# A three-stage kernel on one Trainium2 core: the second MLP's denominator as a linear step squared on GpSimd, and a new order of all instructions

## The chip, the cores and the metric

The kernel runs on one core of a Trainium2 chip. The metric is the device time of one execution in microseconds (us). The kernel before takes 1487.1 us, the median of three runs (1486.95 to 1488.85). A profile of one execution is available. In it PE is TensorE (matmuls; PEld its weight loads), DVE is VectorE, ACT is ScalarE, POOL is GpSimd and SP is SyncE, which issues the transfers. `L949` is line 949 of the kernel.

## What is computed

Attention of 12288 tokens (128 channels) against 768 pooled keys, then two MLPs of 128 to 2048 to 128. The first squares a ReLU, the second applies a rational function P/Q to every element of its hidden layer:

```python
s = scale * (q @ k.T);  a = softmax(s);  x = a @ v          # attention
g = maximum(x @ w1_in, 0) ** 2;          x = g @ w1_out      # first MLP
h = x @ w2_in                                               # second MLP
P = a[0] + a[1] * h + a[2] * h**2 + a[3] * h**3
Q = 1.0 + abs(b[0]) * abs(h) + abs(b[1]) * h**2
out = (P / (Q + 1e-06)) @ w2_out
```

## The kernel before, in words

**Tiling.** The tokens are cut into 25 batches: one of 384, 22 of 512, one of 384 and one of 256. For each batch the work is attention (`attention`), then 16 chunks of the first MLP (`mlp1`, a chunk being 128 rows of the hidden layer), then 8 pairs of chunks of the second MLP (`mlp2`). Most matmuls are done as three fp32r matmuls on high and low parts (L805 to L807 for the input sides, L823 to L825 for the output side of chunks that are split), the rest as one fp32 matmul, which the trace lists as two records (L819).

**The elementwise work of a pair in the second MLP.** With u = |h| from ACT (L944), Q is made in one of two ways. For the pairs in `qpool` (0, 1, 3, 4, 5 and 7) GpSimd makes `K = s1*u + s2` (L947) and then `K = K*u` (L949), and ACT takes `Ln(K + dp)` (L969). For the other two pairs ACT makes `K = (s*u + k1)^2` in one instruction (L952) and takes `Ln(K + da)`. Then ACT makes y0 = exp(-ln) (L970), a first guess of 1/Q, into PSUM. DVE makes P from a square by ACT (L958) with L960, and combines guess and P in three steps: L982 (P times the guess), L984 (Q times the guess) and L987 (one Newton step and the product). Pairs 0 and 3 (`spl`) are split into mH (ACT L997 or DVE L998) and mL (POOL L1000). In the first MLP a chunk goes through ReLU (ACT L847 or DVE L850), a square (POOL L856, in place and of a tile with itself, or ACT L853), and, for split chunks, gH (ACT L865) and gL (POOL L871). L779, L782 and L785 split each MLP's input (x and y) into high and low parts; L785 with `yl` in it is what the second MLP of a batch has to wait for.

**What sets the order.** No loop nest does. `Plan` collects all operations with priorities (a due time by batch and chunk, plus the entry of `off` for the operation's name), penalties for each of two possible engines (`sq_act`, `sq_pool` and the like), the costs `c_dve`, `c_actp`, `c_pool` and so on, the number of buffers (`bufs`) and the most PSUM banks that a kind of tile may hold at once (`caps`; `h2` is the second MLP's hidden layer). `order()` plays them forward and gives one fixed sequence to each engine. On the chip each engine then runs its own sequence strictly in order, waiting on semaphores.

The whole program exists twice, the second time for coefficients out of range (`TERMS`). Only the first (`SQUARES`, `fast`) runs here. The columns of `co_f` hold the coefficients: `k1`, `k2`, `dp`, `da`.

Of the kernel before, what the change touches and what calls it, by code (L numbers as in the profile page):

```python
# [14 lines left out]
ALU = mybir.AluOpType  # L15
# [3 lines left out]
QS = 2.0 ** -20  # L19
QC = QS * (1.0 + 1e-6)  # L20

PE, ACT, DVE, POOL, DMA = "PE", "ACT", "DVE", "POOL", "DMA"
# [10 lines left out]
    hs=[0, 1, 3, 4, 5],  # L33
    lo_dve=60,
    bufs=dict(
        qr=1, qh=1, ql=1, e=4, mn=17, sm=21, aT=1, xh=2, xl=1, yh=2, yl=2, aH=3, aL=2, g1=8, U=2, K=3, Z=7, o=1,
        gH=6, gL=3, mH=1, mL=1,
    ),
    caps=dict(
        h2=6, yb=5, sc=6, st=6, x=1, h1=5, y1=1, y2=1, dc=1,  # L40
    ),
    lead1=17.5,
    leada=18.0,
    d1=3,
    d2=3,
    g=2,
    pair=('kk', 'qp', 'sq2', 'ln', 'y0', 'g0', 'tt', 'rr', 'g2', 'ml', 'mh'),
    rem=[],
    md_act=1,
    md_dve=60,  # L50
    rl_act=8,
    rl_dve=2,
    qh_act=4,
    qh_dve=1,
    spd=[],
    spl=[0, 3],
    qpool=[0, 1, 3, 4, 5, 7],
    sq_act=8,
    sq_pool=0.5,
    gh_act=0.5,  # L60
    gh_dve=60,
    mh_act=8,
    mh_dve=0,
    ml_pool=0,
    ml_dve=60,
    ev_dve=8,
    hi_dve=0,
    rg=1,
    low=4,
    avs=5,  # L70
# [1 line left out]
    head=[384],  # L72
    tail=[384, 256],
    off=dict(
        mh2=-266.25, mh1=-79.25, sc=-10.0, tr=0.75, nr=-368.25, g2=7.0, ex=-137.5, kk=-177.25, rl=-4.75,
        tt=85.5, ev=79.75, mo2=10.5, ln=49.75, g0=-38.25, ab=3.5, sq=184.75, y0=14.75, mn=-278.0, qp=100.0,
        av=-119.5, mo1=4.25, sP=85.5, sq2=132.5, rr=198.5, mh=-16.5, ml=-198.75,
    ),
    free=150.0,
)  # L80
# [10 lines left out]
        qr=1, qh=1, ql=2, e=4, mn=9, sm=5, aT=1, xh=2, xl=2, yh=2, yl=2, aH=3, aL=3, g1=7, U=2, K=2, Z=5, o=1,  # L91
        gH=5, gL=3, mH=3, mL=2,
    ),
    caps=dict(
        dc=6, h2=5, yb=4, sc=5, st=3, x=1, h1=5, y1=1, y2=1,
    ),
    lead1=22.0,
# [5 lines left out]
    rem=[],  # L103
    md_act=0,
    md_dve=0,
    rl_act=2,
    rl_dve=60,
    qh_act=0,
    qh_dve=0.5,
    spd=[],  # L110
    spl=[],
    qpool=[],
    sq_act=4,
    sq_pool=2,
    gh_act=0.5,
# [3 lines left out]
    ml_pool=8,  # L119
    ml_dve=0.5,  # L120
    ev_dve=60,
    hi_dve=1,
# [8 lines left out]
        kk=-27.5, rl=59.75, tt=-37.5, ev=-109.0, mo2=4.25, ln=66.5, g0=-61.0, ab=-105.5, sq=289.5, y0=5.0,  # L131
        mn=-287.5, qp=-77.0, av=-156.0, mo1=5.75,
# [18 lines left out]


def c_mm3(n):
    return 3 * (0.4375 * n + 6)


def c_mm4(n):
# [22 lines left out]

def c_pool(n):
    return 157 + 2.105 * n


def c_pools(n):
# [183 lines left out]
def program(ctx, tc, CFG, fast, co, room, wsr, qT, kvT, w1_in, w1_out, w2_in, w2_out, outT):  # L369

    nc = tc.nc
# [10 lines left out]
    NB = len(sizes)  # L382
# [57 lines left out]
    w_hi = [const.tile([128, DFF], F32R, name=f"w{m}h") for m in range(2)]  # L440
    w_lo = [const.tile([128, DFF], F32R, name=f"w{m}l") for m in range(2)]

    REM, SPL, SPD, QPOOL = CFG["rem"], CFG["spl"], CFG["spd"], CFG["qpool"]
    HS = [[fi for k in ks for fi in (2 * k, 2 * k + 1)] for ks in (CFG["hs"], sorted(REM + SPL + SPD))]
    place = [{fi: n for n, fi in enumerate(x for x in range(NF) if x not in HS[m])} for m in range(2)]
    w_o = [const.tile([128, max(1, len(place[m])), C], F32, name=f"w{m}o") for m in range(2)]
# [439 lines left out]
    def mlp2(b, fp, p):  # L886
        T = sizes[b]
        key = lambda n: [(n, b, fp, e) for e in range(G)]
        hh, yy, uu, ku, zz, mh_, ml_ = (key(n) for n in ("h2", "yb", "U", "K", "Z", "mH", "mL"))
        rem, spl, spd, qpool = fp in REM, fp in SPL, fp in SPD, fp in QPOOL or not fast  # L890

        def add(name, alts, new=None, rd=(), wr=()):

# [48 lines left out]
        def one(name, eng, cost, go, *args, **kw):  # L942
            add(name, [(eng, cost, go, 0)], *args, **kw)
        one("ab", ACT, c_actp, lambda v: act(out=v(uu), in_=v(hh), func=AF.Abs), "U", [hh])  # L944
        if qpool:
            s1, s2 = (QS, co["k2"]) if fast else (co["b"][:, 1:2], co["b"][:, 0:1])
            one("kk", POOL, c_pools, lambda v: ts(  # L947
                out=v(ku), in0=v(uu), scalar1=s1, scalar2=s2, op0=ALU.mult, op1=ALU.add), "K", [uu])
            one("qp", POOL, c_pool, lambda v: nc.gpsimd.tensor_tensor(  # L949
                out=v(ku), in0=v(ku), in1=v(uu), op=ALU.mult), None, [uu], [ku])  # L950
        else:
            one("sq2", ACT, ptr(c_acts), lambda v: act(  # L952
                out=v(ku), in_=v(uu), func=AF.Square, scale=QS ** 0.5, bias=co["k1"]), "K", [uu])
        dl = (co["dp"] if qpool else co["da"]) if fast else QC
        dl_ap = dl if fast else co["qc"]
        c_dl = ptr(c_dve) if fast else c_dve
        if fast:
            one("sP", ACT, ptr(c_actp), lambda v: act(  # L958
                out=v(zz), in_=v(hh), func=AF.Square, bias=co["c"]), "Z", [hh])
# [118 lines left out]
@with_exitstack  # L1078
def attn_moe_moe(
    ctx: ExitStack,  # L1080
    tc: tile.TileContext,
    qT: bass.AP,
    kvT: bass.AP,
    w_sr: bass.AP,
    w1_in: bass.AP,
    w1_out: bass.AP,
    w2_in: bass.AP,
    w2_out: bass.AP,
    pa: bass.AP,
    pb: bass.AP,  # L1090
    outT: bass.AP,
):

    nc = tc.nc
    pool = ctx.enter_context(tc.tile_pool(name="coef", bufs=1))
    wsr = pool.tile([128, w_sr.shape[1]], F32, name="wsr")  # L1100
    room = pool.tile([128, room_size(SQUARES)], F32, name="room")
    col = lambda n, name: pool.tile([128, n], F32, name=name)
    ab, m, r, v, t, w = col(6, "ab"), col(6, "m"), col(2, "r"), col(3, "v"), col(8, "t"), col(6, "w")
    co_f, co_g, flag = col(8, "cf"), col(8, "cg"), pool.tile([128, 1], I32, name="flag")
    c1 = lambda x, n: x[:, n:n + 1]
    nc.sync.dma_start(out=ab[:, 0:4], in_=pa.to_broadcast([128, 4]))
    nc.sync.dma_start(out=ab[:, 4:6], in_=pb.to_broadcast([128, 2]))
    nc.sync.dma_start(out=wsr, in_=w_sr)
    n = KC * kvT.shape[2]
    for c in range(kvT.shape[1] // KC):  # L1110
        nc.sync.dma_start(out=room[:, c * n:(c + 1) * n].rearrange("p (k r) -> p k r", k=KC),
                          in_=kvT[:, c * KC:(c + 1) * KC, :])
    nc.scalar.preload_act_table_set("natural_log_exp_and_others")
    V = nc.vector

    def ts(out, in0, s1, s2, op0, op1=None):
        V.tensor_scalar(out=out, in0=in0, scalar1=s1, scalar2=s2, op0=op0, **({} if op1 is None else dict(op1=op1)))
    MUL, ADD, SUB, MAX, MIN = ALU.mult, ALU.add, ALU.subtract, ALU.max, ALU.min
    GE, LE = ALU.is_ge, ALU.is_le

    V.scalar_tensor_tensor(out=m, in0=ab, scalar=-1.0, in1=ab, op0=MUL, op1=MAX)
    V.tensor_reduce(out=c1(t, 0), in_=m[:, 0:4], axis=AX.X, op=MAX)

    ts(c1(t, 1), c1(t, 0), c1(m, 3), 16.0, MUL, MUL)
    ts(c1(t, 2), c1(m, 2), c1(m, 2), None, MUL)
    V.tensor_tensor(out=c1(w, 0), in0=c1(t, 2), in1=c1(t, 1), op=LE)

    V.scalar_tensor_tensor(out=c1(w, 1), in0=c1(t, 0), scalar=2.0 ** -20, in1=c1(m, 3), op0=MUL, op1=LE)
    ts(c1(w, 2), c1(t, 0), 2.0 ** -40, None, GE)
    ts(c1(w, 3), c1(t, 0), 2.0 ** 40, None, LE)  # L1130

    ts(c1(t, 3), c1(m, 4), c1(m, 4), 0.25, MUL, MUL)
    V.tensor_tensor(out=c1(w, 4), in0=c1(t, 3), in1=c1(m, 5), op=LE)
    ts(c1(t, 4), c1(m, 5), 2.0 ** 10, None, LE)
    V.scalar_tensor_tensor(out=c1(w, 5), in0=c1(m, 5), scalar=2.0 ** -10, in1=c1(t, 4), op0=GE, op1=MUL)
    V.tensor_reduce(out=c1(t, 5), in_=w, axis=AX.X, op=MIN)
    V.tensor_copy(out=flag, in_=c1(t, 5))
    fits = nc.values_load(flag[0:1, 0:1], min_val=0, max_val=1)

    ts(c1(t, 6), c1(t, 5), -1.0, 1.0, MUL, ADD)  # L1140
    V.scalar_tensor_tensor(out=c1(r, 0), in0=c1(ab, 3), scalar=c1(t, 5), in1=c1(t, 6), op0=MUL, op1=ADD)
    V.scalar_tensor_tensor(out=c1(r, 1), in0=c1(m, 5), scalar=c1(t, 5), in1=c1(t, 6), op0=MUL, op1=ADD)
    V.reciprocal(out=r, in_=r)
    ts(v, ab[:, 0:3], c1(r, 0), None, MUL)
    ts(c1(co_f, 0), c1(v, 2), 0.5, None, MUL)
    V.scalar_tensor_tensor(out=c1(co_f, 1), in0=c1(co_f, 0), scalar=c1(co_f, 0), in1=c1(v, 1), op0=MUL, op1=SUB)
    ts(c1(t, 7), c1(m, 4), c1(r, 1), 0.5, MUL, MUL)
    ts(c1(co_f, 2), c1(t, 7), QS ** 0.5, None, MUL)
    ts(c1(co_f, 3), c1(t, 7), 2.0 * QS, None, MUL)
    ts(c1(co_f, 4), c1(r, 1), QC, None, MUL)  # L1150
    V.scalar_tensor_tensor(out=c1(co_f, 5), in0=c1(co_f, 2), scalar=c1(co_f, 2), in1=c1(co_f, 4), op0=MUL, op1=SUB)
    ts(c1(co_f, 5), c1(co_f, 5), -1.0, None, MUL)
    ts(c1(co_f, 6), c1(ab, 3), c1(r, 1), QS, MUL, MUL)

    ts(co_g[:, 0:4], ab[:, 0:4], QS, None, MUL)
    ts(co_g[:, 4:6], m[:, 4:6], QS, None, MUL)
    V.memset(c1(co_g, 6), QC)
    args = (room, wsr, qT, kvT, w1_in, w1_out, w2_in, w2_out, outT)
    with tc.If(fits > 0) as branch:
        with ExitStack() as c:  # L1160
# [46 lines left out]
```

## Time and profile before

| | |
|---|---|
| median of three runs | 1487.1 us |
| the profiled execution | 1486.9 us |
| its span, first to last instruction | 1484.7 us |
| PE busy | 1439.5 us, 97% |
| ACT busy | 1393.4 us, 94% |
| DVE busy | 1386.9 us, 93% |
| POOL busy | 1334.1 us, 90% |

The profiled execution took 2.2 us more than its span. Busy is the time in which an engine has an instruction under way. Matmul records overlap, since a matmul starts before the last has drained; how much work PE is given is therefore read from the distance between the starts of matmuls that follow one another without a wait, and not from their lengths.

### The profile page before, as it was taken

What the parts mean: (1) busy time and instruction counts of PE and PEld (TensorE: products, weight loads), DVE (VectorE), ACT (ScalarE), POOL (GpSimd) and SP (SyncE); (2) the same over time, 40 slices, a digit from 0 to 9 for tenths busy, and PEclk for the clock granted to TensorE, in tenths of its full rate; (3) what the DMA queues carried; (4) which work ended last, traced back from release to release, by engine and by line L of the source; (5) the groups of instructions that cost most, each with busy time, mean ns of one, the idle gap of its engine ahead of it and who ended that gap; (6) DMA issues with size and microseconds to landing.
All of it is one profiled execution on the core that took longest, in us unless ns stands there. A gap on an engine that the chain in (4) does not pass through costs nothing.

```text
span 1484.7 us, 18746 instructions
## 1 busy us (share of the span) xinstructions
PE 1439.5 (97%) x5991; PEld 1053.8 (71%) x5991; DVE 1386.9 (93%) x1857; ACT 1393.4 (94%) x2318; POOL 1334.1 (90%) x1021
## 2 busy tenths in 40 slices
PE   5999999999999999999999999999999999999986
PEld 4887767766767777776777777777777777767764
DVE  7999999999999999999999999999989899989998
ACT  3789989999999999999999999999999999999996
POOL 4789999998999899999998997989999999889984
PEclk8999999999999999999999999999999999999998
DMA  7310000000000000000000000000000000000000
GB/s 283 114 36 8 13 0 15 14 2 8 15 8 15 8 3 13 15 8 8 8 15 8 1 15 15 8 8 15 8 8 8 8 13 1 11 5 3 8 8 12
DMA packets 15549, 28.62 MB, mean 19 GB/s; under 512 B 1745, under 2 KB 6737, under 8 KB 15441
## 3 DMA queue, kind: packets, MB, share of 16 engines
q1 hardware_dynamic: 15440, 27.34, 5.5%
q8 instruction: 49, 0.80, 0.2%
q14 instruction: 60, 0.48, 0.1%
HBM read 21.04 MB, written 6.29 MB: 18 GB/s over the span
## 4 chain that ended last, share of the span: by engine, by line
PE 67%; POOL 13%; ACT 8%; DVE 7%; issue 3%; DMA 1%; SPq 0%; POOLq 0%; ACTq 0%; DVEq 0%
PE psum L819 17%; PE psum L805 9%; PE psum L806 8%; PE psum L807 8%; PE psum L679 4%; PE psum L824 4%; POOL room L949 4%; PE psum L825 4%; PE psum L823 4%; PE psum L720 4%; POOL gL L871 3%; POOL room L947 2%; POOL room L856 2%; PE psum L750 1%; PE psum L749 1%
## 5 line engine op out<-in xcount | busy, mean ns | idle before, releaser
L949 POOL TENSOR_TENSOR room<-room 128x1024 f32<-128x1024 f32 (+2 forms) x150 | 348.3, 2322 | 3.6
L871 POOL TENSOR_TENSOR gL<-room,gH 128x512 fp32r<-128x512 f32 (+2 forms) x250 | 313.0, 1262 | 20.8 <-PE psum L824 15.8
L960 DVE SCALAR_TENSOR_TENSOR room<-room,cf,psum 128x512 f32<-128x512 f32 (+2 forms) x400 | 279.5, 720 | 17.4 <-ACT room L958 15.8
L819 PE MATMUL psum<-room,w1o 128*128 128x512 f32 (+2 forms) x600 | 285.2, 583 | 4.0 <-DVE room L987 4.0
L856 POOL TENSOR_TENSOR room<-room 128x512 f32<-128x512 f32 (+2 forms) x261 | 262.3, 1022 | 12.5 <-ACT room L847 6.6
L982 DVE SCALAR_TENSOR_TENSOR room<-room,v,psum 128x1024 f32<-128x1024 f32 (+2 forms) x200 | 246.1, 1232 | 21.2 <-ACT psum L970 19.4
L958 ACT ACTIVATE room<-psum,cf 128x512 f32<-128x512 f32 (+2 forms) x400 | 262.8, 688 | 0.0
L969 ACT ACTIVATE room<-room,cf 128x1024 f32<-128x1024 f32 (+2 forms) x200 | 226.3, 1132 | 25.4 <-POOL room L949 24.8
L984 DVE SCALAR_TENSOR_TENSOR psum<-room,cf,psum 128x1024 f32<-128x1024 f32 (+2 forms) x200 | 247.5, 1238 | 0.0
L987 DVE SCALAR_TENSOR_TENSOR room<-psum,room 128x1024 f32<-128x1024 f32 (+2 forms) x200 | 235.2, 1177 | 3.1
L944 ACT ACTIVATE room<-psum 128x512 f32<-128x512 f32 (+2 forms) x400 | 223.4, 593 | 12.5 <-PE psum L807 6.5
L947 POOL TENSOR_SCALAR room<-room,cf 128x1024 f32<-128x1024 f32 (+2 forms) x150 | 164.7, 1098 | 48.3 <-ACT room L944 36.0
L970 ACT ACTIVATE psum<-room 128x1024 f32<-128x1024 f32 (+2 forms) x200 | 202.7, 1015 | 0.7 <-DVE room L960 0.3
L805 PE MATMUL psum<-yh,w1h 128*128 128x512 f32 (+2 forms) x400 | 191.2, 478 | 4.8 <-DVE room L987 3.5
L805 PE MATMUL psum<-xh,w0h 128*128 128x512 f32 (+2 forms) x400 | 182.8, 457 | 1.6 <-DVE xh L782 1.2
L819 PEld LDWEIGHTS psum<-room,w1o 128*128 128x128 f32 x600 | 111.1, 192 | 63.1 <-issue 42.9
L806 PE MATMUL psum<-xl,w0h 128*128 128x512 f32 (+2 forms) x400 | 153.4, 383 | 1.5 <-DVE xl L785 1.2
L807 PE MATMUL psum<-yh,w1l 128*128 128x512 f32 (+2 forms) x400 | 154.2, 386 | 0.0
L806 PE MATMUL psum<-yl,w1h 128*128 128x512 f32 (+2 forms) x400 | 153.9, 385 | 0.0
L807 PE MATMUL psum<-xh,w0l 128*128 128x512 f32 (+2 forms) x400 | 153.6, 384 | 0.0
L847 ACT ACTIVATE room<-psum 128x512 f32<-128x512 f32 (+2 forms) x255 | 148.3, 601 | 5.1 <-PE psum L807 3.2
L865 ACT ACTIVATE gH<-room 128x512 fp32r<-128x512 f32 (+2 forms) x250 | 149.8, 632 | 2.9 <-POOL room L856 2.6
(126 smaller groups left out, 3124.4 us busy)
## 6 DMA issues: line engine op xcount, KB each, us to landing
room<-in_kv_dram SPq DMA_DIRECT2D x16, 384.0 KB, 7.8
room<-in_q_dram SPq DMA_DIRECT2D x22, 256.0 KB, 2.6
out_dram<-room SPq DMA_DIRECT2D x22, 256.0 KB, 2.0
room<-in_moe_w_in_dram SPq DMA_DIRECT2D x8, 512.0 KB, 4.6
room<-in_moe_w_out_dram SPq DMA_DIRECT2D x16, 256.0 KB, 2.7
room<-in_q_dram SPq DMA_DIRECT2D x2, 192.0 KB, 4.7
out_dram<-room SPq DMA_DIRECT2D x2, 192.0 KB, 1.9
room<-in_q_dram SPq DMA_DIRECT2D x1, 128.0 KB, 2.0
```

What stands on the lines that cost most here:

```text
L805: nc.tensor.matmul(out=out, lhsT=w_hi[m][:, sl], rhs=hi, start=True, stop=False)
L806: nc.tensor.matmul(out=out, lhsT=w_hi[m][:, sl], rhs=lo, start=False, stop=False)
L807: nc.tensor.matmul(out=out, lhsT=w_lo[m][:, sl], rhs=hi, start=False, stop=True)
L819: nc.tensor.matmul(out=o, lhsT=w_o[m][:, place[m][fi], :], rhs=rhs(), start=first, stop=last)
L856: nc.gpsimd.tensor_tensor(out=G(), in0=G(), in1=G(), op=ALU.mult)
L871: nc.gpsimd.tensor_tensor(out=mk("gL", gl)[:, :T], in0=G(), in1=f(tiles[gh][:, :T]), op=ALU.subtract)
L949: one("qp", POOL, c_pool, lambda v: nc.gpsimd.tensor_tensor(out=v(ku), in0=v(ku), in1=v(uu), op=ALU.mult), None, [uu], [ku])
L958: one("sP", ACT, ptr(c_actp), lambda v: act(out=v(zz), in_=v(hh), func=AF.Square, bias=co["c"]), "Z", [hh])
L960: one("z3", DVE, ptr(c_dve), lambda v: stt(out=v(zz), in0=v(zz), scalar=co["nd"], in1=v(hh), op0=ALU.subtract, op1=ALU.mult), None, [hh], ...
L982: one("g0", DVE, ptr(c_dve), lambda v: stt(out=v(zz), in0=v(zz), scalar=e0, in1=v(yy), op0=ALU.add, op1=ALU.mult), None, [yy], [zz])
L984: one("tt", DVE, c_dl, lambda v: stt(out=v(yy), in0=v(ku), scalar=dl, in1=v(yy), op0=ALU.add, op1=ALU.mult), None, [ku], [yy])
L987: one("g2", DVE, c_dve, lambda v: stt(out=v(g_), in0=v(yy), scalar=2.0, in1=v(zz), op0=ALU.subtract, op1=ALU.mult, reverse0=True), None, [ ...
```

## The change

In the second MLP the two GpSimd steps of a pair become `K = sqrt(QS)*u + k1` and `K = K*K`: the second step takes one tile twice where it took two tiles. The constant that is left to `Ln` and to L984 is then `da` for all pairs, and `k2` and `dp` go (the column of `dp` is kept, since `da` is made from it). The number of instructions of a pair stays. The first step keeps its form, one multiplication and one addition per element.

The pairs that take the GpSimd way in the last two batches (384 and 256 tokens) are `qtail` (0, 3, 4, 5, 6 and 7): pair 6 in the place of pair 1.

The planner has a new cost for the second step (`c_poolq`), and its numbers are new: penalties, due times, buffers, caps. `c_mm3` gets a lower bound of 110, which no size of this kernel reaches.

```diff
-        qr=1, qh=1, ql=1, e=4, mn=17, sm=21, aT=1, ...
-        gH=6, gL=3, mH=1, mL=1,
+        qr=1, qh=1, ql=1, e=5, mn=27, sm=29, aT=1, ...
+        gH=5, gL=3, mH=1, mL=1,
-        h2=6, yb=5, sc=6, st=6, x=1, h1=5, y1=1, y2=1, dc=1,
+        h2=4, yb=6, sc=6, st=5, x=1, h1=6, y1=1, y2=1, dc=1,
-    lead1=17.5,
+    lead1=20.5,
+    qtail=[0, 3, 4, 5, 6, 7],
-    sq_act=8,
-    sq_pool=0.5,
+    sq_act=0,
+    sq_pool=8,
...
-        mh2=-266.25, mh1=-79.25, ...
+        mh2=-164.5, mh1=-75.5, ...
...
+def c_poolq(n):
+    return 1.96 * n + 10
...
-        rem, spl, spd, qpool = fp in REM, fp in SPL, fp in SPD, fp in QPOOL or not fast
+        rem, spl, spd, qpool = fp in REM, fp in SPL, fp in SPD, not fast or fp in (QPOOL if b < NB - 2 else QTAIL)
...
-            s1, s2 = (QS, co["k2"]) if fast else (co["b"][:, 1:2], co["b"][:, 0:1])
+            s1, s2 = (QS ** 0.5, co["k1"]) if fast else (co["b"][:, 1:2], co["b"][:, 0:1])
...
-            one("qp", POOL, c_pool, lambda v: nc.gpsimd.tensor_tensor(
-                out=v(ku), in0=v(ku), in1=v(uu), op=ALU.mult), None, [uu], [ku])
+            qf = ku if fast else uu
+            one("qp", POOL, c_poolq if fast else c_pool, lambda v: nc.gpsimd.tensor_tensor(
+                out=v(ku), in0=v(ku), in1=v(qf), op=ALU.mult), None, [uu], [ku])
...
-        dl = (co["dp"] if qpool else co["da"]) if fast else QC
+        dl = co["da"] if fast else QC
```

**POOL, in the middle of the program, before** (a row is a line, an operation, out<-in and its size; x3 stands for three alike in a row; `room` holds most working tiles):

```order
L947 TENSOR_SCALAR room<-room,cf 128x1024
L856 TENSOR_TENSOR room<-room 128x512
L949 TENSOR_TENSOR room<-room 128x1024
L871 TENSOR_TENSOR gL<-room,gH 128x512
L947 TENSOR_SCALAR room<-room,cf 128x1024
L856 TENSOR_TENSOR room<-room 128x512
L949 TENSOR_TENSOR room<-room 128x1024
L871 TENSOR_TENSOR gL<-room,gH 128x512 x2
L856 TENSOR_TENSOR room<-room 128x512 x3
L1000 TENSOR_TENSOR mL<-room,mH 128x1024
```

Now, at about the same place (L953 and L956 are the two steps of Q, L862 the first MLP's square, L877 gL):

```order
L953 TENSOR_SCALAR room<-room,cf 128x1024
L877 TENSOR_TENSOR gL<-room,gH 128x512
L956 TENSOR_TENSOR room<-room 128x1024
L877 TENSOR_TENSOR gL<-room,gH 128x512
L862 TENSOR_TENSOR room<-room 128x512
L953 TENSOR_SCALAR room<-room,cf 128x1024
L877 TENSOR_TENSOR gL<-room,gH 128x512
L956 TENSOR_TENSOR room<-room 128x1024
L862 TENSOR_TENSOR room<-room 128x512
L877 TENSOR_TENSOR gL<-room,gH 128x512
L862 TENSOR_TENSOR room<-room 128x512
L1007 TENSOR_TENSOR mL<-room,mH 128x1024
```

The kinds of instructions are the same; other work now stands between the two steps of Q, and over the whole program 22 more squares of 512 columns stand on POOL and 22 fewer on ACT.

**DVE at the end, before**, from the split of the last batch's y (256 tokens) on; the rows of 384 belong to the batch ahead of it:

```order
L785 TENSOR_TENSOR yl<-psum,yh 128x256
L984 SCALAR_TENSOR_TENSOR psum<-room,cf,psum 128x2x384
L960 SCALAR_TENSOR_TENSOR room<-room,cf,psum 128x384 x2
L987 SCALAR_TENSOR_TENSOR room<-psum,room 128x2x384
L982 SCALAR_TENSOR_TENSOR room<-room,v,psum 128x2x384
L984 SCALAR_TENSOR_TENSOR psum<-room,cf,psum 128x2x384
L987 SCALAR_TENSOR_TENSOR room<-psum,room 128x2x384
L982 SCALAR_TENSOR_TENSOR room<-room,v,psum 128x2x384
L960 SCALAR_TENSOR_TENSOR room<-room,cf,psum 128x384 x2
L984 SCALAR_TENSOR_TENSOR psum<-room,cf,psum 128x2x384
L987 SCALAR_TENSOR_TENSOR room<-psum,room 128x2x384
L982 SCALAR_TENSOR_TENSOR room<-room,v,psum 128x2x384
```

Now (L791 is that split; L967, L989, L991 and L994 are L960, L982, L984 and L987):

```order
L791 TENSOR_TENSOR yl<-psum,yh 128x256
L991 SCALAR_TENSOR_TENSOR psum<-room,cf,psum 128x2x384
L967 SCALAR_TENSOR_TENSOR room<-room,cf,psum 128x384 x2
L994 SCALAR_TENSOR_TENSOR room<-psum,room 128x2x384
L989 SCALAR_TENSOR_TENSOR room<-room,v,psum 128x2x384
L991 SCALAR_TENSOR_TENSOR psum<-room,cf,psum 128x2x384
L994 SCALAR_TENSOR_TENSOR room<-psum,room 128x2x384
L989 SCALAR_TENSOR_TENSOR room<-room,v,psum 128x2x384
L967 SCALAR_TENSOR_TENSOR room<-room,cf,psum 128x256 x3
L991 SCALAR_TENSOR_TENSOR psum<-room,cf,psum 128x2x384
L989 SCALAR_TENSOR_TENSOR room<-room,v,psum 128x2x256
```

Behind the split stood 6 pairs' worth of L984 and of L987 at 384 columns, 5 of L982, 8 of L960 and one cast (L998); now it is 3, 3, 2, 2 and none. The rest stands ahead of the split. Those of 256 columns, all behind it, are the same in number. On PE likewise: behind the last output matmul of the first MLP, 12 chunks of the batch of 384 still had their input matmuls to come (L805 to L807), now 2.

## Rows read from the trace of the kernel before

**Rows 1.** The page: span and busy time of each engine

```profile
span 1484.7 us, 18746 instructions
PE 1439.5 (97%) x5991; PEld 1053.8 (71%) x5991; DVE 1386.9 (93%) x1857; ACT 1393.4 (94%) x2318; POOL 1334.1 (90%) x1021
```

**Rows 2.** Stretches: their length, each engine's busy us (instructions), then the granted clock

```profile
0.00:47.40 47.40, 28.54 (x141) 24.76 (x141) 38.95 (x96) 18.47 (x36) 21.15 (x27) 0.86 0.66 236
47.40:107.60 60.20, 59.67 (x301) 50.83 (x302) 58.15 (x131) 53.13 (x115) 52.45 (x56) 1.00 0.26 82
107.60:1412.00 1304.40, 1295.93 (x5316) 936.89 (x5315) 1226.00 (x1541) 1262.91 (x2049) 1215.02 (x898) 1.00 0.03 9
1412.00:1432.90 20.90, 20.09 (x103) 15.88 (x102) 19.59 (x25) 19.93 (x42) 20.28 (x22) 1.00 0.04 13
1432.90:1484.70 51.80, 35.27 (x135) 25.48 (x133) 44.21 (x68) 38.98 (x81) 25.22 (x22) 0.82 0.03 9
1469.70:1480.00 10.30, 7.93 (x23) 6.10 (x24) 9.37 (x16) 5.89 (x12) 3.19 (x3) 0.51 0.01 2
```

**Rows 3.** The timeline of PE in the middle: start, length, instruction

```profile
610.79 0.60 PE L720 MATMUL psum<-ident,room 128*128 128x128 f32 x4
611.23 1.88 PE L819 MATMUL psum<-room,w1o 128*128 128x512 f32 x4
...
700.28 0.39 PE L807 MATMUL psum<-yh,w1l 128*128 128x512 f32 x1
700.50 0.39 PE L805 MATMUL psum<-yh,w1h 128*128 128x512 f32 x1
...
709.64 1.88 PE L819 MATMUL psum<-room,w1o 128*128 128x512 f32 x4
710.96 0.80 PE L823 MATMUL psum<-gH,w0oh 128*128 128x512 f32 x1
711.59 0.40 PE L824 MATMUL psum<-gL,w0oh 128*128 128x512 f32 x1
```

**Rows 4.** POOL's and ACT's groups by shape: count, busy us, mean ns, idle before

```profile
L949 POOL TENSOR_TENSOR room<-room 128x1024 f32<-128x1024 f32 x132 | 318.5, 2413 | 2.7
L871 POOL TENSOR_TENSOR gL<-room,gH 128x512 fp32r<-128x512 f32 x220 | 284.6, 1304 | 18.2 <-PE psum L824 14.5
L856 POOL TENSOR_TENSOR room<-room 128x512 f32<-128x512 f32 x232 | 241.5, 1057 | 12.3 <-ACT room L847 6.6 <-DVE room L850 1.9
L949 POOL TENSOR_TENSOR room<-room 128x512 f32<-128x512 f32 x6 | 7.7, 1286 | 0.5
L856 POOL TENSOR_TENSOR room<-room 128x256 f32<-128x256 f32 x14 | 8.6, 637 | 0.2
L853 ACT ACTIVATE room<-room 128x512 f32<-128x512 f32 x120 | 74.6, 649 | 1.0 <-DVE room L850 0.8
```

**Rows 5.** Waits: engine, line, whom it waited for; us in total, times, longest

```profile
ACT room L969 <- POOL room L949: 24.8, 43, 1.7
PEld psum L805 <- DVE room L960: 12.1, 35, 1.2
PE psum L819 <- DVE room L987: 4.0, 4, 1.3
```

**Rows 6.** The timeline of DVE near the end: start, length, instruction, idle before

```profile
1433.17 0.42 DVE L785 TENSOR_TENSOR yl<-psum,yh 128x256 fp32r<-128x256 f32 x1
1433.51 1.01 DVE L984 SCALAR_TENSOR_TENSOR psum<-room,cf,psum 128x768 f32<-128x768 f32 x1
1434.43 0.61 DVE L960 SCALAR_TENSOR_TENSOR room<-room,cf,psum 128x384 f32<-128x384 f32 x1
1435.20 0.61 DVE L960 SCALAR_TENSOR_TENSOR room<-room,cf,psum 128x384 f32<-128x384 f32 x1 [0.16 <-ACT room L958]
1435.73 0.95 DVE L987 SCALAR_TENSOR_TENSOR room<-psum,room 128x768 f32<-128x768 f32 x1
1436.60 1.00 DVE L982 SCALAR_TENSOR_TENSOR room<-room,v,psum 128x768 f32<-128x768 f32 x1
```

More of the change, by code (lines that the diff above doesn't have):

```diff
@@ L35 @@
     bufs=dict(
-        qr=1, qh=1, ql=1, e=4, mn=17, sm=21, aT=1, xh=2, xl=1, yh=2, yl=2, aH=3, aL=2, g1=8, U=2, K=3, Z=7, o=1,
-        gH=6, gL=3, mH=1, mL=1,
+        qr=1, qh=1, ql=1, e=5, mn=27, sm=29, aT=1, xh=2, xl=1, yh=2, yl=2, aH=3, aL=2, g1=8, U=2, K=3, Z=7, o=1,
+        gH=5, gL=3, mH=1, mL=1,
     ),
     caps=dict(
-        h2=6, yb=5, sc=6, st=6, x=1, h1=5, y1=1, y2=1, dc=1,
+        h2=4, yb=6, sc=6, st=5, x=1, h1=6, y1=1, y2=1, dc=1,
     ),
-    lead1=17.5,
+    lead1=20.5,
     leada=18.0,
@@ L48 @@
     rem=[],
-    md_act=1,
-    md_dve=60,
-    rl_act=8,
+    md_act=60,
+    md_dve=0.5,
+    rl_act=0,
     rl_dve=2,
     qh_act=4,
-    qh_dve=1,
+    qh_dve=0.5,
     spd=[],
@@ L63 @@
     mh_dve=0,
-    ml_pool=0,
+    ml_pool=2,
     ml_dve=60,
     ev_dve=8,
-    hi_dve=0,
+    hi_dve=1,
     rg=1,
@@ L74 @@
     off=dict(
-        mh2=-266.25, mh1=-79.25, sc=-10.0, tr=0.75, nr=-368.25, g2=7.0, ex=-137.5, kk=-177.25, rl=-4.75,
-        tt=85.5, ev=79.75, mo2=10.5, ln=49.75, g0=-38.25, ab=3.5, sq=184.75, y0=14.75, mn=-278.0, qp=100.0,
-        av=-119.5, mo1=4.25, sP=85.5, sq2=132.5, rr=198.5, mh=-16.5, ml=-198.75,
+        mh2=-164.5, mh1=-75.5, sc=-71.0, tr=1.0, nr=-376.25, g2=37.0, ex=-126.75, kk=-258.0, rl=23.75, tt=120.0,
+        ev=33.75, mo2=10.5, ln=114.25, g0=-10.5, ab=-80.5, sq=186.75, y0=-21.5, mn=-380.5, qp=185.5, av=-140.25,
+        mo1=3.0, sP=130.0, sq2=158.5, rr=199.75, mh=-170.25, ml=-210.25,
     ),
@@ L112 @@
     qpool=[],
+    qtail=[],
     sq_act=4,
@@ L153, in c_mm3 @@
 def c_mm3(n):
-    return 3 * (0.4375 * n + 6)
+    return 3 * max(0.4375 * n + 6, 110)
 def c_mm4(n):
@@ L441, in program @@
     w_lo = [const.tile([128, DFF], F32R, name=f"w{m}l") for m in range(2)]
-    REM, SPL, SPD, QPOOL = CFG["rem"], CFG["spl"], CFG["spd"], CFG["qpool"]
+    REM, SPL, SPD, QPOOL, QTAIL = CFG["rem"], CFG["spl"], CFG["spd"], CFG["qpool"], CFG["qtail"]
     HS = [[fi for k in ks for fi in (2 * k, 2 * k + 1)] for ks in (CFG["hs"], sorted(REM + SPL + SPD))]
@@ L1148, in attn_moe_moe @@
     ts(c1(co_f, 2), c1(t, 7), QS ** 0.5, None, MUL)
-    ts(c1(co_f, 3), c1(t, 7), 2.0 * QS, None, MUL)
     ts(c1(co_f, 4), c1(r, 1), QC, None, MUL)
@@ L1160, in attn_moe_moe @@
         with ExitStack() as c:
-            co = dict(c=c1(co_f, 0), nd=c1(co_f, 1), e=c1(v, 0), k1=c1(co_f, 2), k2=c1(co_f, 3), dp=c1(co_f, 4),
+            co = dict(c=c1(co_f, 0), nd=c1(co_f, 1), e=c1(v, 0), k1=c1(co_f, 2),
                       da=c1(co_f, 5), out=c1(co_f, 6))
```

## The prediction, made before the changed kernel was run

> **What bounds the kernel now.** I read the busy times first, then stretches of the span, then single instructions. The page [rows 1] shows four engines at 90 to 97%, PE ahead. That alone doesn't say how much can be won, so the next question is how much matmul work there is. The timeline of PE in the middle [rows 3] gives the distance between starts: an fp32r matmul of 512 columns follows the last after 0.22 to 0.23 us (0.229 is the middle of many), two fp32 matmuls (four records) take 711.59 - 0.23 - 709.64 = 1.72 us, 0.86 each, and four transposes 0.44. A full batch has 153 of the first (48 for each MLP's input, 30 and 12 for split outputs, 15 for attention), 19 of the second, 24 score matmuls of 384 columns (0.17 each, by columns) and 24 transposes: 35.0 + 16.3 + 4.1 + 2.6 = 58 us. All batches and the start come to 1405 us. The span is 1484.7, so PE is without work for 80 us, and no change that leaves the matmuls alone, as this one does, can win more.
>
> Where the 80 are: I cut the order of PE at the first matmul of the second MLP of batch 0 (107.6 us in the trace) and of batch 23 (1412.0). Ahead of the first stand 79.5 us of work, so 28 are lost. Between them stand 1282.2, and the stretch [rows 2] takes 1304.4, so 22 are lost (its record-based idle time is only 8.5, since drawn-out matmul records cover the small gaps). Behind stand 43.2, and 72.7 pass, so 29.5 are lost. In the first stretches the clock is granted at 0.86 and DVE and the transfers set the pace; in the middle PE is busy for 99.4%, ACT for 97%, DVE for 94%, POOL for 93%; from 1432.9 on PE is busy for 35 of 52 us, while DVE is for 44 [rows 2]. So: PE bounds the middle, with ACT close behind it, and DVE bounds the end, where only the second MLP is left and PE waits for L987 [rows 5].
>
> **The square on GpSimd.** 132 of the 150 second steps (L949) have 1024 columns and take 2.41 us [rows 4]. The new step multiplies a tile with itself, at a size that the trace doesn't show. The nearest row is the first MLP's square, L856, 1.06 us at 512 and 0.64 at 256, where L949 needs 1.29 at 512. Going on by that slope gives 1.06 + 2 x 0.42 = 1.90; by L949's own growth from 512 to 1024 (x 1.88) 1.98; doubled 2.11. I take 1.95, between the two that use a measured growth. Saved: 132 x 0.46 = 61 us, and about 6 on the 18 smaller ones; bounds 132 x 0.30 = 40 and 132 x 0.51 = 67, and the smaller ones.
>
> At 512 columns [rows 4] show that for POOL a product of a tile with itself is cheaper than one of two tiles, by 0.23 of 1.29 us at 512. The Trainium skill (GPSIMD Engine Reference, section 2.1) says otherwise of a two-input operation: its two read streams take turns on one physical port, and about 2.5 cycles per element is the floor; a square reads two streams too. By that sentence the saving would be nothing, and it has its place among the rivals.
>
> **Squares moved from ACT to POOL.** The order has 22 more L856 of 512 columns and 4 of 384: 22 x 1.06 + 4 x 0.8 = 26 us more on POOL, and 22 x 0.62 (74.6 / 120, rows 4) + 2 = 15.5 us less on ACT, of which 2 come back by other small swaps. The casts that change sides between ACT and DVE (12 splits of x and y to DVE, 4 each of qh and mH to ACT) nearly cancel. Sums: POOL 1334 - 67 + 26 = 1293, ACT 1393 - 13 = 1380, DVE 1387 as before, PE the same 1405. So the engine that bounds the end gets no shorter; ACT, which crowds PE in the middle, does, and POOL most.
>
> **The middle.** ACT waits for L949 in 43 places, 24.8 us in all [rows 5]; each can shrink by up to 0.46 us, 20 at most, where ACT had been idle only 41 us of the stretch. But PE has only 22 us to win there, in hundreds of small gaps, and of those the larger ones that I could put down to someone are shared by ACT, DVE and POOL. A quarter of the 22 is my estimate: -5 us. Bounds: -12, about half of it, as the most that two relieved engines can return; +4, a fifth more, since all queues are new and have their own wrong places, which nothing in a trace of before can show.
>
> **The end.** This is the term with a place. In the order DVE has, behind the split of the last y, three L984, three L987, three L982, six L960 and a cast fewer, all of 384 columns or pairs of it. From start to start they take 0.92, 0.87, about 0.95 and 0.53 us [rows 6], the cast about 0.9: 2.8 + 2.6 + 2.9 + 3.2 + 0.9 = 12.4 us less, from 43.4 to 31.0 us of DVE's work. That stretch took 51.8 us [rows 2] with 8 us of waiting; with the same waiting it takes 39.4. The work has gone ahead of the split, beside first-MLP matmuls, where DVE has room (busy 94%) and PE is the bound; PE has 6.8 us more there (ten chunks' input matmuls, 30 x 0.17, and some outputs). Net -5.6, so -6 with the 0.24 us by which each of the last steps on POOL shrinks. The lower bound is from another cut: from the first second-MLP matmul of batch 23 on, DVE's own work goes from 61.1 to 59.2 and PE's ahead of it from 1361.7 to 1361.0: -2.6. The upper bound is -8: at 1469.7 to 1480.0 PE's granted clock is 0.51 [rows 2], the lower of its two levels (1.2 GHz), behind a stretch in which PE had often waited, and part of that could go. Pair 6 in the place of pair 1 in the last two batches changes no sum: 6 pairs on POOL either way.
>
> **The start.** The order puts one more tile of scores ahead of the first MLP (21.4 us of PE's work instead of 20.3), in a stretch where PE waits for the first batch's attention anyhow: -1, bounds -3 and +2. Transfers: the same 98 rows on SP; in the middle they use 3% of the engines [rows 2], so they move at no cost. Buffers: one more `e`, one `gH` less, at most 4 banks for `h2`; the last is a rival below.
>
> **Sum.** Against the profiled execution of 1486.9 us: -1 - 5 - 6 = -12, so 1474.9; the median is 0.2 above it. Forecast 1475, from 1465 (-3 - 12 - 8 is -23; not all at once) to 1484.
>
> **Rivals.**
> - **ACT takes DVE's place at the end**, and the middle keeps its gaps. From the cut at batch 23 on, ACT's work by rows goes from 57.3 to 59.0 us, as long as DVE's 59.2, and the two hand each pair to and fro (L958 to L960, L970 to L982), so two full engines fit worse than one. Against it: ahead of the last y's split both now have more done. It would give -1 to -3, about 1485.
> - **Slower: PSUM for the second MLP's input.** With at most four banks for `h2` the matmuls of a third pair wait until DVE has done L960 of the first. Before, with six, weight loads at L805 waited for L960 in 35 places, 12.1 us, 0.35 each [rows 5]. If each of the 200 pairs waits so, 70 us of waiting stand there, of which matmuls still under way cover most; a fourth uncovered is 18 us, and against -6 at the end 1499; 12 uncovered give 1493. It decides from 0.06 us of uncovered wait per pair on. Against it: PE's queue holds other work ahead (first MLP, attention) at nearly every such place, and the order was made with the cap in it.
> - **The square costs as much as the product.** Then POOL has 1334 + 26 = 1360 us, close to ACT's 1380, and each Ln starts 0.46 us later than the order counts on. The middle gains nothing, loses perhaps 1, and the end stays: 1486.9 - 6 = about 1481. [Rows 4] at 512 columns speak against it. (It is what that sentence of the Trainium skill's GPSIMD Engine Reference, section 2.1, would do here.)
>
> **How the numbers follow.** Forecast 0.65, ACT at the end 0.16, `h2` 0.12, square as dear as the product 0.07. A measurement here can tell about 0.2%, 3 us, from no change: faster is below 1484.1, slower above 1490.1. Faster: 0.62 of the forecast, 0.05 of the first rival and 0.05 of the third, 0.72. Same: 0.03 + 0.11 + 0.02 = 0.16. Slower: 0.12. Range 1466 to 1488: it takes in the forecast but for its lower end (0.06) and the rivals but for `h2`.
>
> **What would show it.** The new step at 1.90 to 2.11 us for 1024 columns, POOL near 1293 and ACT near 1380 us busy, DVE unchanged. The first second-MLP matmul of batch 23 near 1406 instead of 1412. From the last y's split to the end 38 to 41 us instead of 51.8. ACT's wait for the second step well under 24.8. The forecast is wrong if the stretch behind the split stays near 50 us, if L805 waits for L960 in far more than 35 places, or if the middle's 22 us grow; then the new order, and not the square, has set the time.

## The result, and the profile after

The changed kernel takes 1470.8 us (median of 4 runs, 1470.1 to 1471.1) against 1487.2 before (4 runs): ratio 0.9886, 95% interval 0.9874 to 0.9899, 16.4 us less. Its profiled execution took 1470.7 us, 1.9 more than its span. The page, with busy time and then the shares of the chain of work that ended last (followed back from the last instruction, at each step to what released it):

```profile
span 1468.8 us, 18714 instructions
PE 1430.0 (97%) x5991; PEld 1052.3 (72%) x5991; DVE 1384.4 (94%) x1862; ACT 1384.7 (94%) x2289; POOL 1276.7 (87%) x1044
...
PE 88%; DVE 5%; ACT 3%; DMA 1%; issue 1%; POOL 1%; SPq 0%; DVEq 0%; ACTq 0%; POOLq 0%
```

The chain's line of the kernel before, which the prediction didn't use:

```profile
PE 67%; POOL 13%; ACT 8%; DVE 7%; issue 3%; DMA 1%; SPq 0%; POOLq 0%; ACTq 0%; DVEq 0%
```

Compared with [rows 1] POOL has lost 57 us of busy time, ACT 9 and DVE 2.5. The chain shows a larger shift: POOL's share of it falls from 13% to 1%, and PE's rises from 67% to 88%.

Stretches of the kernel after, to be laid beside [rows 2] (length; then busy us of PE, PEld, DVE, ACT and POOL with their instructions; then the granted clock):

```profile
0.00:104.00 104.00, 85.45 (x435) 72.66 (x436) 94.19 (x221) 73.28 (x155) 75.64 (x84) 0.97 0.47 157
104.00:1396.00 1292.00, 1291.14 (x5317) 940.30 (x5316) 1227.04 (x1551) 1251.20 (x2012) 1159.00 (x917) 1.00 0.03 9
1396.00:1428.50 32.50, 28.63 (x136) 21.18 (x135) 31.71 (x41) 31.85 (x64) 25.85 (x29) 1.00 0.02 9
1428.50:1468.80 40.30, 24.75 (x108) 18.13 (x106) 31.46 (x52) 28.41 (x62) 16.20 (x17) 0.85 0.04 11
```

In the middle (104.00 to 1396.00) the idle time between PE's records is 0.9 us, where it was 8.5. POOL's share there is 90% (1159.0 of 1292.0), where it was 93%.

To compare sequences I use the measure of the prediction: the time at which the first second-MLP matmul of batch 0 and of batch 23 starts, less the matmul work that PE's sequence has ahead of it at the measured distances between starts. That gives PE's lost time at the start, in the middle, and at the end. "Old" and "new" are the sequences of the kernels before and after.

| kernel | time, us | start | middle | end |
|---|---|---|---|---|
| before | 1487.2 | 28.0 | 22.2 | 29.3 |
| after | 1470.8 | 26.4 | 8.6 | 28.7 |
| e2: old sequence, new step | 1475.0 | 28.6 | 11.1 | 28.2 |
| e9: old sequence, old step, POOL relieved elsewhere | 1476.5 | 28.9 | 12.0 | 28.4 |
| e1: new sequence, old step | 1513.1 | 26.4 | 50.1 | 29.1 |
| e3: old numbers, new step, planned anew | 1497.6 | 28.1 | 31.4 | 30.3 |
| e4: new, pair 1 for pair 6 at the end | 1473.0 | 27.1 | 8.8 | 31.0 |
| e6: new, half of DVE's L991 at the end | 1470.6 | 26.3 | 8.6 | 28.6 |
| e7: new, half of ACT's Ln at the end | 1468.7 | 26.9 | 8.6 | 26.1 |
| e8: new, both | 1468.0 | 26.3 | 8.9 | 25.2 |

Of the 16 us, 13.6 are from the middle, some 1.6 from the start, and under 1 from the end. Each row is one execution. How far two executions differ by themselves shows in e11 below, whose edit touches the last two batches alone: its middle comes out 0.9 us shorter than that of the kernel before, so differences of 1 us in these columns say little.

### The profile page after: what moved, and what is told of

Same layout as the page of the kernel before. It is cut to its first block, busy times and chain, and to the rows that moved or that the text cites. A ratio compares the mean times of both kernels' runs of the same rounds, so it can differ in the third digit from the quotient of the medians.

```text
span 1468.8 us, 18714 instructions
## 1 busy us (share of the span) xinstructions
PE 1430.0 (97%) x5991; PEld 1052.3 (72%) x5991; DVE 1384.4 (94%) x1862; ACT 1384.7 (94%) x2289; POOL 1276.7 (87%) x1044
## 4 chain that ended last, share of the span: by engine, by line
PE 88%; DVE 5%; ACT 3%; DMA 1%; issue 1%; POOL 1%; SPq 0%; DVEq 0%; ACTq 0%; POOLq 0%
PE psum L825 23%; PE psum L811 11%; PE psum L813 11%; PE psum L812 11%; PE psum L685 6%; PE psum L830 5%; PE psum L829 5%; PE psum L831 5%; PE psum L726 4%; PE psum L756 2%; PE psum L755 2%; PE psum L757 2%; PE psum L759 1%; DMA room<-in_kv_dram 1%; DVE room L967 1%
## 5 line engine op out<-in xcount | busy, mean ns | idle before, releaser
L877 POOL TENSOR_TENSOR gL<-room,gH 128x512 fp32r<-128x512 f32 (+2 forms) x250 | 312.1, 1259 | 37.5 <-PE psum L830 29.1
L862 POOL TENSOR_TENSOR room<-room 128x512 f32<-128x512 f32 (+2 forms) x287 | 287.7, 1018 | 36.2 <-ACT room L853 20.7
L967 DVE SCALAR_TENSOR_TENSOR room<-room,cf,psum 128x512 f32<-128x512 f32 (+2 forms) x400 | 279.2, 719 | 9.1 <-ACT room L965 7.1
L825 PE MATMUL psum<-room,w1o 128*128 128x512 f32 (+2 forms) x600 | 282.1, 579 | 5.7 <-DVE room L994 5.7
L956 POOL TENSOR_TENSOR room<-room 128x1024 f32<-128x1024 f32 (+2 forms) x150 | 274.9, 1833 | 2.6
L989 DVE SCALAR_TENSOR_TENSOR room<-room,v,psum 128x1024 f32<-128x1024 f32 (+2 forms) x200 | 246.1, 1232 | 17.3 <-ACT psum L977 16.6
L991 DVE SCALAR_TENSOR_TENSOR psum<-room,cf,psum 128x1024 f32<-128x1024 f32 (+2 forms) x200 | 247.4, 1237 | 0.0
L950 ACT ACTIVATE room<-psum 128x512 f32<-128x512 f32 (+2 forms) x400 | 222.9, 584 | 18.7 <-PE psum L813 13.2
L994 DVE SCALAR_TENSOR_TENSOR room<-psum,room 128x1024 f32<-128x1024 f32 (+2 forms) x200 | 235.1, 1176 | 2.6
L953 POOL TENSOR_SCALAR room<-room,cf 128x1024 f32<-128x1024 f32 (+2 forms) x150 | 164.5, 1097 | 48.6 <-ACT room L950 47.6
L811 PE MATMUL psum<-yh,w1h 128*128 128x512 f32 (+2 forms) x400 | 189.8, 475 | 6.2 <-DVE room L994 4.0
L811 PE MATMUL psum<-xh,w0h 128*128 128x512 f32 (+2 forms) x400 | 179.1, 448 | 0.2 <-DVE room L994 0.2
```

The costliest lines, as they stand in the source:

```text
L811: nc.tensor.matmul(out=out, lhsT=w_hi[m][:, sl], rhs=hi, start=True, stop=False)
L825: nc.tensor.matmul(out=o, lhsT=w_o[m][:, place[m][fi], :], rhs=rhs(), start=first, stop=last)
L862: nc.gpsimd.tensor_tensor(out=G(), in0=G(), in1=G(), op=ALU.mult)
L877: nc.gpsimd.tensor_tensor(out=mk("gL", gl)[:, :T], in0=G(), in1=f(tiles[gh][:, :T]), op=ALU.subtract)
L956: one("qp", POOL, c_poolq if fast else c_pool, lambda v: nc.gpsimd.tensor_tensor(out=v(ku), in0=v(ku), in1=v(qf), op=ALU.mult), None, [uu] ...
L967: one("z3", DVE, ptr(c_dve), lambda v: stt(out=v(zz), in0=v(zz), scalar=co["nd"], in1=v(hh), op0=ALU.subtract, op1=ALU.mult), None, [hh], ...
```

## The experiments

### Which of the two won the middle: the cheaper step or the new sequence

Two kernels cross the two halves of the change. In e1 and e2 every engine has the same instructions in the same places as the kernel from which it is made; only the operands of the two steps of Q (and their constants) differ. (e1 has one more DVE instruction of a single column at the start, which makes `k2` again.) The planner keeps the cost that it had, so nothing moves.

e2, from the kernel before:

```diff
-            s1, s2 = (QS, co["k2"]) if fast else ...
+            s1, s2 = (QS ** 0.5, co["k1"]) if fast else ...
...
-                out=v(ku), in0=v(ku), in1=v(uu), op=ALU.mult), None, [uu], [ku])
+                out=v(ku), in0=v(ku), in1=v(ku if fast else uu), op=ALU.mult), None, [uu], [ku])
...
-        dl = (co["dp"] if qpool else co["da"]) if fast else QC
+        dl = co["da"] if fast else QC
```

> The kernel before with every engine's sequence as it was, and only the second step of Q on GpSimd as the square. Theory A (the cheaper step): ACT's wait for that step falls from 24.8 us to under 6, the middle's lost 22 us fall to 9 to 13, and the time is 1474 to 1479. Theory B (the new sequence): 1484 to 1487.

Measured: 1475.0 us (1474.6 to 1475.8), ratio 0.9915 (0.9898 to 0.9931). Its groups by shape have the step at 1908 ns (busy us, mean ns):

```profile
L949 POOL TENSOR_TENSOR room<-room 128x1024 f32<-128x1024 f32 x132 | 251.8, 1908 | 2.5
```

Its waits have ACT's for that step (us in total, times, longest):

```profile
ACT room L969 <- POOL room L949: 3.1, 6, 1.0
```

Its chain, and in the next fence its middle, as a stretch with the columns as above:

```profile
PE 85%; DVE 8%; ACT 3%; DMA 1%; issue 1%; POOL 1%; SPq 0%; DVEq 0%; ACTq 0%; POOLq 0%
```

```profile
107.60:1401.50 1293.90, 1290.37 (x5319) 939.64 (x5318) 1224.97 (x1542) 1265.74 (x2050) 1141.03 (x900) 1.00 0.03 9
```

The step alone, in a sequence that was searched for the dearer one, brings 12.2 of the 16.4 us, nearly all in the middle (22.2 to 11.1). ACT does as much work as before (1265.7 against 1262.9, rows 2), its wait falls from 24.8 us [rows 5] to 3.1, and POOL's share of the chain from 13% to 1%. Theory A holds.

e1, from the kernel after, is the other way round:

```diff
-            s1, s2 = (QS ** 0.5, co["k1"]) if fast else ...
+            s1, s2 = (QS, co["k2"]) if fast else ...
...
-            qf = ku if fast else uu
+            qf = uu
...
-        dl = co["da"] if fast else QC
+        dl = (co["dp"] if qpool else co["da"]) if fast else QC
...
```

> The changed kernel with every engine's sequence as it is, and only the second step of Q on GpSimd as before (a product of two tiles, 2.41 us at 1024 columns instead of 1.90). Theory A, the cheaper step won the middle's 13.6 us: the middle loses most of that again, since the sequence counts on 1.90, and the time is 1481 to 1490. Theory B, the new sequence won it: the 67 us of POOL's time come out of its idle time, and the time is 1471 to 1475.

Measured: 1513.1 us (1512.7 to 1515.4), ratio 1.0176 (1.0159 to 1.0193). Both theories had it too low. The page has this chain:

```profile
PE 52%; POOL 25%; ACT 9%; issue 7%; DVE 6%; DMA 1%; SPq 0%; POOLq 0%; ACTq 0%; DVEq 0%
```

The waits have ACT's for the step:

```profile
ACT room L976 <- POOL room L956: 60.4, 85, 2.0
```

And the middle, as a stretch:

```profile
104.00:1437.60 1333.60, 1312.85 (x5318) 933.08 (x5316) 1230.78 (x1551) 1251.01 (x2011) 1233.63 (x917) 1.00 0.03 9
```

The direction is A's: half a microsecond more per step, and PE loses 50 us in the middle instead of 8.6. The size shows that the new sequence is not a better one in itself, but one for the cheaper step. It puts 22 more squares on POOL, whose share of the chain is 25% here; whether those squares make the loss or other parts of the sequence, e1 does not tell. With the dear step the new sequence is 26 us worse than the old one, with the cheap step 4.3 better (1475.0 to 1470.8, of which about 2 each at the start and in the middle).

### POOL's load, or the way through POOL to Ln

The cheaper step does two things: it takes work off POOL, and it shortens the way from |h| to Ln in each pair. e9 takes a like time off POOL at another place, in the kernel before, and leaves both steps of Q as they were: the first MLP's squares on POOL are done on 11 of 16 of their columns, the rest is left unsquared.

```diff
         def sq_p():
-            nc.gpsimd.tensor_tensor(out=G(), in0=G(), in1=G(), op=ALU.mult)
+            w = T * 11 // 16
+            nc.gpsimd.tensor_tensor(out=G()[:, :w], in0=G()[:, :w], in1=G()[:, :w], op=ALU.mult)
```

> The kernel before with every engine's sequence and the two-tile step of Q as it was; the first MLP's squares on GpSimd are done on 11 of 16 of their columns (the rest is left unsquared), which takes about 67 us off POOL, as much as the cheaper step of Q does, but off another chain. Theory L (POOL's load): 1475 to 1478, like the kernel before with the square. Theory C (the chain from POOL's second step to ACT's Ln to DVE and PE): 1482 to 1487, and ACT's wait for L949 stays near 20 us.

Measured: 1476.5 us (1476.0 to 1477.7), ratio 0.9928 (0.9912 to 0.9945). Its lines stand one further down, so that L950 is the second step of Q, L948 the first and L945 the |h|. Its waits and, in the next fence, its middle as a stretch:

```profile
ACT room L970 <- POOL room L950: 7.9, 13, 1.5
POOL room L948 <- ACT room L945: 56.5, 54, 3.6
```

```profile
107.60:1402.60 1295.00, 1291.16 (x5320) 939.60 (x5319) 1227.22 (x1543) 1265.56 (x2051) 1150.80 (x899) 1.00 0.03 9
```

Two waits of the kernel before, to be laid beside them:

```profile
POOL room L947 <- ACT room L944: 36.0, 29, 3.6
ACT gH L865 <- POOL room L856: 2.6, 6, 0.7
```

Theory L holds. POOL's busy time over the whole program falls from 1334.1 to 1267.3 us here and to 1254.8 in e2: 67 us off POOL are worth 10.7 us, and 79 are worth 12.2. ACT's wait for the second step shrinks to 7.9 us although the step is as long as before. It starts earlier: POOL now reaches the first step before its |h| is there 54 times and not 29. That the way through the square itself got shorter can hardly be the reason, since gH had waited for squares on POOL for 2.6 us in all. So POOL, at a busy share of 93%, stood behind about half of what PE lost in the middle of the kernel before. ACT, at 97%, did not hold up that half, for its work is the same in both runs. What the other half is due to was not tested: no run takes work off ACT or DVE in the middle with the sequence kept.

### A sequence planned for the new cost but not searched

e3 is e2 with the planner told of the cost (`c_poolq`), all its other numbers as before.

```diff
-            one("qp", POOL, c_pool, lambda v: ...
+            one("qp", POOL, c_poolq if fast else c_pool, lambda v: ...
```

> The kernel before with the square and with the planner told its cost, all other numbers of the planner as before: the sequence is made anew, but not searched. Theory A: near the kernel before's sequence with the square, 1472 to 1480. Theory B, it takes numbers searched for it: 1483 to 1492.

Measured: 1497.6 us (1497.3 to 1498.5), ratio 1.0069 (1.0052 to 1.0085). It has the same instructions for Q as e2, and loses 31.4 us in the middle instead of 11.1: a better cost in the planner, without new numbers, gave a sequence that is 22.6 us worse than leaving the old one. It is nearer to B, and slower than either theory had it. Its chain:

```profile
PE 82%; DVE 9%; ACT 4%; issue 2%; POOL 1%; DMA 1%; SPq 0%; DVEq 0%; ACTq 0%; POOLq 0%
```

POOL is out of the chain here as in e2, so the 31.4 us are not POOL's load; what in the sequence costs them stays open. The searched numbers of the changed kernel give a sequence that is 27 us faster than this one and 4.3 faster than e2's.

### What bounds the end

The prediction held that DVE bounds it. e6, e7 and e8 leave out half of one instruction per pair, on DVE, on ACT, or on both, in the last two batches alone and with every engine's sequence kept:

```diff
+        part = (lambda a: a[:, :, :T // 2] if b >= NB - 2 else a)
e6, e8:
-                out=v(yy), in0=v(ku), scalar=dl, in1=v(yy), op0=ALU.add, op1=ALU.mult), ...
+                out=part(v(yy)), in0=part(v(ku)), scalar=dl, in1=part(v(yy)), op0=ALU.add, op1=ALU.mult), ...
e7, e8:
-        one("ln", ACT, ptr(c_acts), lambda v: act(out=v(uu), in_=v(ku), func=AF.Ln, bias=dl_ap), ...
+        one("ln", ACT, ptr(c_acts), lambda v: act(out=part(v(uu)), in_=part(v(ku)), func=AF.Ln, bias=dl_ap), ...
```

> The changed kernel, sequences as they are; in the last two batches DVE's L991 is done on half of the columns only (the other half of that step is left out): about 5.4 us less on DVE there. If DVE alone bounds the end: 1466 to 1467. If ACT and DVE bound it in turns: 1468 to 1470.

> The changed kernel, sequences as they are; in the last two batches ACT's Ln (L976) is done on half of the columns only (the other half of that step is left out): about 4.9 us less on ACT there. If DVE alone bounds the end: 1470 to 1471, no change. If ACT and DVE bound it in turns: 1468 to 1470.

> The changed kernel, sequences as they are, with both: in the last two batches DVE's L991 and ACT's Ln on half of the columns only. If DVE alone bounds the end, the same as with DVE's half: 1466 to 1467. If ACT and DVE bound it in turns, more than the sum of the two: 1463 to 1466.

Measured: e6 1470.6 us (1469.7 to 1473.1), e7 1468.7 (1468.3 to 1469.8), e8 1468.0 (1467.4 to 1468.6), against 1470.8 of the changed kernel. The stretch from the first second-MLP matmul of batch 23 to the split of the last y, as it is in e6 (columns as above):

```profile
1396.00:1428.50 32.50, 28.63 (x137) 21.32 (x136) 30.06 (x41) 31.87 (x64) 25.86 (x29) 1.00 0.02 9
```

The same stretch in e7:

```profile
1396.00:1428.50 32.50, 28.77 (x137) 21.28 (x137) 32.02 (x43) 31.03 (x64) 26.27 (x29) 1.00 0.02 9
```

In e6 DVE had 1.7 us less to do there, and ACT stayed full (31.87 of 32.50): nothing moved. Over the whole program DVE was busy for 4.8 us less in e6 (1379.6 against 1384.4) and got 0.2 us for it. ACT was busy for 3.7 us less in e7 (1381.0 against 1384.7), and that returned 2.1 us; both together returned 2.8. So in the changed kernel ACT bounds the end more than DVE does. (Half a Ln also shortens the way from Ln to the guess and on to DVE; these runs do not part that from ACT's load.) "DVE alone" is wrong; "in turns" is wrong for e6 and fits e7, and e8 fell short of what it asked for (1463 to 1466).

The same two cuts on the kernel before (L984 and L969 there):

> The kernel before, sequences as they were; in the last two batches DVE's L984 is done on half of the columns only (the other half of that step is left out): about 5.4 us less on DVE. If DVE bounded the end of the kernel before, as the prediction has it: 1482 to 1484. If ACT did: 1486 to 1488, no change.

> The kernel before, sequences as they were; in the last two batches ACT's Ln (L969) is done on half of the columns only (the other half of that step is left out): about 4.9 us less on ACT. If DVE bounded the end: 1486 to 1488, no change. If ACT did: 1483 to 1485.

Measured: e10 1486.9 us (ratio 0.9996, 0.9986 to 1.0005), e11 1486.4 (0.9991, 0.9981 to 1.0000), ten runs each, against 1488.3 of the kernel before in 19 runs beside them. DVE was busy for 4.1 us less in e10 (1382.8 against 1386.9) and ACT for 4.5 less in e11 (1388.9 against 1393.4), and both times agree with no change and miss what was expected of an engine that bounds. So neither engine by itself is shown to bound the end of the kernel before. What does, the hand-over from one to the other or the sequence itself, these runs leave open, since both at once was not tried on that kernel.

### Which pairs go through GpSimd at the end

e4 has `qtail=[0, 1, 3, 4, 5, 7]`, e12 `[0, 2, 3, 4, 5, 6, 7]`, e5 all eight; the sequences differ from the changed kernel's in the last two batches alone.

> The changed kernel with pair 1 in the place of pair 6 again on GpSimd in the last two batches; all engines' sequences are the same until those batches. If the choice of pairs matters, the last stretch grows by 1 us or more (1472 to 1475); by my sums, six pairs on GpSimd either way, it does not: 1470 to 1472.

> The changed kernel with all eight pairs of the last two batches on GpSimd: two squares per batch (L959) less on ACT, 3.4 us, and 8 us more on POOL, which is busy for half of the last 49 us. If ACT bounds the end: 1468 to 1470, unless the sequence, which is made anew for these batches alone, is worse. If it does not: 1470 to 1473.

> The changed kernel with seven pairs of the last two batches on GpSimd (all but pair 1): half of that, 1.7 us less on ACT. If ACT bounds the end: 1469 to 1470; if it does not: 1470 to 1472.

Measured: e4 1473.0 us (1471.4 to 1474.1; ratio 0.9898, 0.9881 to 0.9914), e5 1471.7 (ratio 0.9895, 0.9878 to 0.9911), e12 1471.6 (ratio 0.9894, 0.9877 to 0.9910); the changed kernel's ratio is 0.9886. All four runs of e4 lie above the four of the changed kernel, though the intervals of the ratios overlap, and its end is 2.3 us longer in the trace (31.0 against 28.7), which is that of its slowest run. So the pair chosen probably counts a little, though six pairs go either way: the planner makes another sequence from it. e5 and e12 say nothing of ACT, because the relief did not come about: ACT is busy for 1383.6 us in e5 and 1384.7 in e12, against 1384.7, and DVE for 1.6 and 1.0 us more than the 1384.4 of the changed kernel. None of these versions beats the changed kernel.

## Why the prediction was right, and where it was not

The forecast was 1475, the range 1466 to 1488; it is 1470.8. The sum is right to 4 us, and that is partly luck: two of its terms erred against each other, the middle by 8.6 us too little and the end by some 5 too much.

- **The step's price: right.** It took 1.90 us at 1024 columns, the growth of L856 from 256 to 512 carried on; I had taken 1.95. POOL's sum of 1293 us came out at 1276.7. From the groups by shape of the kernel after, and in the next fence its waits:

```profile
L956 POOL TENSOR_TENSOR room<-room 128x1024 f32<-128x1024 f32 x132 | 250.7, 1901 | 1.7
```

```profile
ACT room L976 <- POOL room L956: 2.8, 5, 0.9
```

  The third rival, the square as dear as the product, is out. The two-input floor of the Trainium skill (GPSIMD Engine Reference, section 2.1), about 2.5 cycles per element, would be some 2.1 us at 1024 columns at the 1.2 GHz of that page's section 1, an estimate. The trace disagrees for a tile with itself: 1.90 us at 1024 columns, and 1.49 where the same estimate gives 1.6 at 768; at 512 (1.04 against 1.07) the two nearly meet, and at 256 (0.64, L862, against 0.53) the trace lies above.

- **The middle: right in that the cheaper step wins there, wrong in the engine behind it and in the size**, and its bound missed: -5 forecast, -12 the bound, -13.6 measured. The step that failed is "A quarter of the 22 is my estimate". I had shared PE's small gaps out by who ended them and ranked the engines by busy share, ACT ahead. e2 and e9 show that POOL's load alone stood behind half of the 22. The chain's line shown above, POOL 13% where ACT had 8% and DVE 7%, pointed there. That each of ACT's waits for the step "can shrink by up to 0.46 us, 20 at most" gave no bound either: the waits went from 24.8 to 2.8 us, and in e9 to 7.9 with the step as long as before, because the work ahead of the step counts as well as the step.

- **The squares moved to POOL:** I counted them as a relief of ACT, the engine close behind PE. ACT's busy time fell by 9 us (13 forecast), and e2 has its gain with none of that. They are 26 us more on POOL, which the cheaper step pays for; that they by themselves make e1's loss is not shown.

- **The end: wrong.** -6 forecast with -2.6 as its smaller bound, -0.6 to -0.8 measured. The stretch from the last y's split to the end did shrink as worked out, to 40 us (39.4 forecast, 51.8 before). The split in the timeline of DVE after:

```profile
1428.72 0.42 DVE L791 TENSOR_TENSOR yl<-psum,yh 128x256 fp32r<-128x256 f32 x1
```

  But the stretch ahead of it, from the first second-MLP matmul of batch 23, grew from 21 to 32.5 us, where I had added only PE's 6.8. The step that failed is "beside first-MLP matmuls, where DVE has room (busy 94%)". The rows had it otherwise: of the 20.90 us from 1412.00 to 1432.90 DVE was idle for 1.3 [rows 2], and PE's 6.8 more make 8.1 us of room for 12.4 us of work. After the change DVE is busy for 31.71 and ACT for 31.85 of 32.50 us, 12 us more each, and up to the last output matmul of the first MLP PE lost 6.9 us, where it had lost 1.9. The work was moved into a stretch that could not take it without growing. The cut that gave the smaller bound, -2.6, had counted this: from batch 23 on DVE's own work hardly changes. Nor was DVE shown to bound the end to begin with (e10). One count was wrong as well: behind the last output matmul of the first MLP, the trace before has 8 chunks of the batch of 384 with their input matmuls to come, and not 12, so PE's work moved ahead is some 7.5 us. The first rival, ACT in DVE's place at the end, fits e6 and e7 for this part, together with a middle that it did not foresee.

- **"Changes no sum"** for pair 6 in the place of pair 1: true of the sum, but e4 is 2.2 us slower; the sequence that follows from it probably matters.

- **The start:** -1 forecast, -1.6 measured, within its bounds; no run tests the reason given.

- **The `h2` rival** did not come. Weight loads at L811 waited for L967 about as often as before [rows 5], in the waits of the kernel after:

```profile
PEld psum L811 <- DVE room L967: 11.9, 33, 1.0
```

## What to carry to other kernels

With in-order queues on five engines the one with the highest busy share behind the bound need not be the one that costs time: look at the chain, and try a relief of each engine with the sequence frozen. Separate a cheaper instruction from the new sequence that comes with it by crossing the two; here the new sequence alone costs 26 us and with the cheaper step gains 4. When work is moved ahead into another stretch, set it in us against the idle time of the stretch that receives it.

## What was not expected of the hardware

On GpSimd a product of a tile with itself is cheaper than one of two tiles at each of the three sizes at which both were seen, and saves more the longer the row: 1.04 against 1.29 us at 512 columns, 1.49 against 1.84 at 768, 1.90 against 2.41 at 1024. The second step of Q at 768 and 512 columns, after and (at 768; the others are in rows 4) before:

```profile
L956 POOL TENSOR_TENSOR room<-room 128x768 f32<-128x768 f32 x12 | 17.9, 1493 | 0.4
L956 POOL TENSOR_TENSOR room<-room 128x512 f32<-128x512 f32 x6 | 6.2, 1040 | 0.5
L949 POOL TENSOR_TENSOR room<-room 128x768 f32<-128x768 f32 x12 | 22.1, 1843 | 0.4
```
